# Attention and experts on one core: a unit's value products in two groups instead of three, a wider transposition of its maxima, and a new steady order

## The chip, the core and the metric

One Trainium2 chip, one of its cores. The time is device time of one execution in microseconds (us); lower is better. The kernel before took 1059.7 us (median of three runs, 1058.65 to 1059.89).

## What is computed

An attention layer whose output is the input of a mixture of eight experts, of which each token goes to one. Batch 8, 12 heads, 448 positions, head width 64; the experts have 768 inputs, 1024 hidden units and 768 outputs; 3584 tokens.

```
q_n, k_n = rmsnorm(q, g_q), rmsnorm(k, g_k)
scores = q_n @ k_n.T / sqrt(64);  scores -= scores.max(-1)
attn = exp(scores);  attn /= attn.sum(-1) + 1e-9
x = (attn @ v) with the heads side by side         # 3584 x 768
logits = x @ w_gate + modality_bias[modality_id]
e = argmax(logits);  g = softmax(logits)[e]
out[token] = g * (relu(x[token] @ w1[e]) @ w2[e])
```

## The kernel before, in words

**Units and slots.** The attention runs over 48 units; a unit is two heads of one batch. Both heads' 448 keys together are 896 rows, that is seven chunks of 128 (j = 0 to 6); chunk 3 holds the last 64 keys of the first head and the first 64 of the second. The main loop counts slots n = 7 u + j. In slot (u, j) the score products `st` of unit u for chunk j are issued (transposed: keys on partitions; two matmuls, four for chunk 3), and beside them work of other units: the products `sa` of unit u + 2, of which only the row maxima are wanted (queries on partitions, `PLAN['sa']` = 14 slots ahead); the turning `tr` of q and k of units three and four ahead; `mt`, which turns a unit's maxima; `av`, the products with the values of the unit before; `sums` and `gates`, which add the row sums of exp and the gate logits of four units in one PSUM tile `pm`; `sp` (in `recips`) and `xt`, which turn sums, logits and outputs back. `rt` are two small matmuls of the routing of a finished batch.

**What each engine has in a unit.** TensorE (PE): the above. ScalarE (ACT): exp of every `st`, the casts of turned q and k into their places, squares for the norms, copies of `av` and `pm`. VectorE (DVE): a maximum for every `sa` tile, the low halves of q and k (the products run in fp32r with a high and a low part), one product-add of the row sums, the scaling of `xt`, the routing. GpSimd (POOL): the rest of the row sums (`csum`), the two norms, and routing DMAs. SyncE issues loads and the moves of the halves.

**Value products.** For unit u, `av(u, c)` with c = 0, 1, 2 takes whole chunks: per head a 128 x 64 weight tile, head 0 writes output rows 0 to 63 and head 1 rows 64 to 127, so the array works as two halves of 64 columns. c = 3 takes the two halves of chunk 3, with 64 rows and 64 columns each. The numbers are fp32, so each of these matmuls shows as two in the trace: four `MATMUL` per c. `PLAN['av']` = (1, 1, 4, 6) says in which slot of the next unit each c is issued. One PSUM tile (`ps_o`, one buffer) takes them; `avcopy` on ACT empties it in the slot after c = 3.

**Maxima.** DVE writes the negated maxima of a unit into the seven columns of `mx`; `mt` (`PE.transpose(ps[0:NJ, :128], t["mx"], idn)`, L871) turns 128 x 7 into 7 x 128, ACT copies seven rows, a DMA moves them into the row of `ql` that subtracts them in the score products.

**Order.** Nothing is scheduled by a tool on these engines: `PLAN` says for every kind of work how many slots ahead of its unit it is issued (`tk`, `tq` turning; `nq`, `nk` norms; `sk`, `sq` squares; `rs` reciprocal roots; `ld` loads), `first` holds exceptions for the first units, `pdef` says in which of the next slots ACT's and DVE's parts of a `tr` come (even: at a slot's end, odd: at its start), `csd` and `cse` the same for the parts of `csum`, `pmp`/`pmpa` how many routing operations a slot takes, `sml` the slot of `sums` from unit 36 on, `xr`, `x0` and `w10` when tokens and weights of the first expert slot are fetched and turned. Each engine then does its instructions in that order, and semaphores make them wait for each other. PSUM has two buffers for `st`, two for `sa`, two that `tr`, `mt`, `xt`, `sp` and `rt` share.

**Experts.** Fourteen expert slots of 256 tokens follow: first products `ph` (144 matmuls of 256 columns), second products `py` (96 of 384), with steps 24 s + b; the table `MOE` says in which step which piece of the next slot's weights is fetched (`w1`, `w2`) or split into high and low part (`s1`, `s2`), and when its tokens are turned (`xtr`) and lists read (`get`, `fin`).

Of the kernel before, what the change touches and what calls it, by code (L numbers as in the profile page):

```python
# [13 lines left out]
ALU = mybir.AluOpType  # L14
# [7 lines left out]
NJ = 7  # L22
# [45 lines left out]
def kernel(  # L68
# [16 lines left out]
    PE, SY = nc.tensor, nc.sync  # L85
# [314 lines left out]
    def view(t, off, p, *dims):  # L400
        n = 1
        for d in dims:
            n *= d
        a = t[:p, off : off + n]
        if len(dims) > 1:
            ax = " ".join("abcd"[: len(dims)])
            a = a.rearrange(f"p ({ax}) -> p {ax}", **dict(zip("abcd"[1:], dims[1:])))
        return a
# [37 lines left out]
    sw, SS = at_g, W + LG  # L446
    ss_b, ry_b = ([view(sw, SS + 48 * (2 * o + i), CP, 2, 6 * NCH) for i in range(2)] for o in range(2))
    ra_b, rz_b = SS + 48 * 4, SS + 48 * 5
    mx_b = [view(sw, SS + 288 + 8 * i, 128, NJ) for i in range(2)]
    rs_b = [cp.tile([CP, NCH, 4, 2], F32, name=f"rs{i}") for i in range(2)]  # L450
    xt_0 = [view(r2w, o, 128, 2, TB) for o in (PW + VW + W, PW, PW + 512)]
    xg, xt_m = xrw[:, 0 : 2 * DM], view(xrw, 2 * DM, 128, 6, TB)
# [221 lines left out]

    if True:
        zt = view(yw, 0, 128, NE * NT * 2 // 128)
        for z in zeros + qm_b:
            V.memset(z.bitcast(F32), 0.0)
        HB = {}
# [188 lines left out]
        def mt(u):  # L868
            t = T[u]
            ps = ps_t.tile([128, 512], F32, tag="t", name=f"mt{u}")  # L870
            PE.transpose(ps[0:NJ, :128], t["mx"], idn)  # L871

            def act():
                ms = ms_b[u % 2]
                A.copy(ms, ps[0:NJ, :128])
                (A if u in PLAN["ma"] else SY).dma_start(t["ql"][64:65].rearrange("p h s -> p (h s)").bitcast(F32),
                            ms.bitcast(F32))

            return act
# [16 lines left out]
        def csum(u, h):  # L896
            t = T[u]
            if h == 0:
                t["cs"] = cs_b[u % 3]
            p = t["p"]  # L900
            c2 = c2_b[:, h]

            if h in CSV:
                V.scalar_tensor_tensor(out=c2, in0=p[:, 3], scalar=half[:, h : h + 1], in1=p[:, 4 * h],
                                       op0=ALU.mult, op1=ALU.add)
            else:
                G.tensor_tensor(out=c2, in0=p[:, 0], in1=p[:, 1], op=ALU.add)

            def more():
                if h in CSV:  # L910
                    G.tensor_tensor(out=c2, in0=c2, in1=p[:, 4 * h + 1], op=ALU.add)
                else:
                    G.tensor_tensor(out=c2[LO], in0=c2[LO], in1=p[LO, 3], op=ALU.add)

            def rest():
                G.tensor_tensor(out=t["cs"][:, h], in0=c2, in1=p[:, 4 * h + 2], op=ALU.add)

            return more, rest
# [610 lines left out]
```

## Time and profile before

| what | value |
|---|---|
| median of three runs | 1059.7 us |
| the profiled execution's own time | 1058.66 us |
| its span in the profile | 1056.9 us |
| TensorE busy | 1035.4 us, 98% |
| VectorE, ScalarE, GpSimd busy | 738.5, 698.5, 737.4 us |
| attention, first `st` to the first `ph` | 34.6 to 555.9 us |
| experts | 555.9 us to the end |

The profiled execution lies 1.0 us under the median, so a time that is reckoned from it stands 1 us lower than one reckoned from the median. A busy TensorE is one with a matmul somewhere in its pipeline; how fast it goes is read from the distance of one matmul's start to the next.

### The profile page before, as it was taken

How to read it: one execution, taken by the hardware profiler on the slowest of the kernel's cores; microseconds unless marked ns; L12 is line 12 of the kernel's file. 1: busy time of each engine (PE TensorE's matmuls, PEld its weight loads, DVE VectorE, ACT ScalarE, POOL GpSimd, SP SyncE). 2: the span in 40 equal slices, each digit the busy share in tenths (PEclk: the TensorE clock that was granted, in tenths of full speed). 3: DMA queues.
4: the chain of work that ended last, by engine and by line, in shares of the span. 5: the costliest groups of instructions: out<-in, count | busy, mean ns of one | idle time of the engine just before them, and what ended most of it. 6: DMA issues, size and time to landing. Idle time of an engine off the chain costs nothing.

```text
span 1056.9 us, 19700 instructions
## 1 busy us (share of the span) xinstructions
PE 1035.4 (98%) x6463; PEld 819.1 (78%) x6463; DVE 738.5 (70%) x1398; ACT 698.5 (66%) x1409; POOL 737.4 (70%) x743
## 2 busy tenths in 40 slices
PE   8899999999999999999999999999999999999996
PEld 7655566655666556665557999999999999999996
DVE  8787777877778777787687985756656665566640
ACT  6788888878888788887655554655555555555540
POOL 5897776787867878778876768665575556655531
PEclk8999999999999999999999999999999999999999
DMA  8766767787677877775735102111163111111170
GB/s 209 162 165 149 193 144 178 170 167 183 145 178 167 170 167 158 164 166 135 204 103 198 39 27 63 44 50 47 45 217 124 44 53 46 61 31 47 45 273 34
DMA packets 137156, 131.17 MB, mean 124 GB/s; under 512 B 75228, under 2 KB 130752, under 8 KB 135892
## 3 DMA queue, kind: packets, MB, share of 16 engines
q1 hardware_dynamic: 113188, 88.73, 36.1%
q0 software_dynamic: 23856, 41.08, 12.1%
q8 instruction: 53, 0.87, 0.4%
q14 instruction: 59, 0.48, 0.2%
HBM read 138.72 MB, written 22.38 MB: 152 GB/s over the span
## 4 chain that ended last, share of the span: by engine, by line
PE 86%; DVE 5%; DMA 2%; issue 2%; ACT 2%; POOL 1%; SPq 1%; POOLq 0%; ACTq 0%; DVEq 0%
PE ph L525 20%; PE py L556 19%; PE st L888 16%; PE av L927 15%; PE sa L860 5%; PE tr L773 3%; PE pm L942 2%; PE xt L984 2%; PE pm L949 1%; DMA l_d<-ltb,posi 1%; PE sa L851 1%; DVE w1w L53 1%; DVE at_hlw L53 1%; DVE w2lw L53 1%; DVE xw L53 1%
## 5 line engine op out<-in xcount | busy, mean ns | idle before, releaser
L53 DVE TENSOR_REDUCE at_hlw<-sa 128x1 f32<-128x448 f32 x336 | 203.2, 617 | 67.5 <-PE sa L860 64.6
L525 PEld LDWEIGHTS ph<-xw,w1w 128*128 128x128 f32 x2016 | 244.7, 192 | 4.1 <-issue 2.8
L525 PE MATMUL ph<-xw,w1w 128*128 128x256 f32 x2016 | 246.9, 284 | 0.6 <-DVE hlw L53 0.3
L888 PE MATMUL st<-w1w 128*128 128x448 f32 (+1 forms) x480 | 172.3, 408 | 2.3 <-ACT at_w2lw L53 2.0
L53 POOL DMA_INDIRECT xrw<-x_d,i x112 | 146.6, 1309 | 33.1 <-issue 31.7
L888 PEld LDWEIGHTS st<-w1w 128*128 128x128 f32 (+1 forms) x480 | 84.2, 189 | 102.6 <-ACT xw L53 38.1
L53 DVE TENSOR_TENSOR w1w<-r,w1w 128x512 fp32r<-128x512 f32 (+1 forms) x180 | 114.7, 678 | 15.7 <-ACT w1w L53 15.5
L53 ACT ACTIVATE r2w<-st 128x448 f32<-128x448 f32 x168 | 90.2, 539 | 52.6 <-PE st L888 46.6
L53 POOL TENSOR_TENSOR r2w<-r2w 128x448 f32<-128x448 f32 (+1 forms) x72 | 82.3, 1143 | 50.0 <-DVE r2w L53 21.5
L556 PE MATMUL py<-w2lw,hhw 128*128 128x384 f32 x448 | 115.0, 334 | 0.0
L53 ACT CAST w1w<-r 128x512 fp32r<-128x512 f32 (+1 forms) x180 | 103.1, 629 | 11.6 <-DMA r<-in_moe_w_dram,tb_w1i 8.5
L53 ACT ACTIVATE hhw<-ph 128x512 fp32r<-128x512 f32 x56 | 33.5, 598 | 114.6 <-PE ph L525 114.6
L53 ACT CAST w1w<-xw 64x448 fp32r<-64x448 f32 x188 | 105.7, 562 | 5.0 <-DVE xw L53 1.1
L860 PE MATMUL sa<-w1w 128*128 128x448 f32 x282 | 104.7, 373 | 3.4 <-DVE at_hlw L53 3.1
L53 ACT ACTIVATE at_w2lw<-st 128x448 f32<-128x448 f32 x168 | 90.3, 539 | 23.4 <-PE st L888 18.2
L888 PE MATMUL st<-w1w,w2ha 65*128 65x448 f32 x288 | 100.6, 370 | 0.0
L53 POOL DMA_INDIRECT out_dram<-yw,lb_oi x22 | 22.8, 1038 | 99.5 <-ACT yw L53 89.7
L53 POOL TENSOR_TENSOR xrw<-r,at_hlw 112x512 f32<-112x512 f32 x89 | 91.1, 1043 | 0.2
L556 PEld LDWEIGHTS py<-w2lw,hhw 128*128 128x128 f32 x448 | 81.0, 188 | 0.0
L53 POOL TENSOR_TENSOR r2w<-r2w,at_w2lw 64x448 f32<-64x448 f32 (+1 forms) x48 | 54.7, 1139 | 34.8 <-DVE rs L53 14.7
L53 DVE TENSOR_TENSOR w2lw<-r2w,w2ha 128x1536 fp32r<-128x1536 f32 x28 | 49.2, 1757 | 39.7 <-ACT w2ha L53 36.3
L53 DVE SCALAR_TENSOR_TENSOR hlw<-ph,hhw 128x512 fp32r<-128x512 f32 x56 | 38.6, 690 | 49.8 <-ACT hhw L53 47.0
(304 smaller groups left out, 2166.4 us busy)
## 6 DMA issues: line engine op xcount, KB each, us to landing
w1w<-xw SPq DMA_DIRECT2D x312, 112.0 KB
r<-in_q_dram SPq DMA_DIRECT2D x48, 224.0 KB
r<-in_k_dram SPq DMA_DIRECT2D x48, 224.0 KB
w2ha<-xw SPq DMA_DIRECT2D x72, 112.0 KB
r2w<-in_v_dram SPq DMA_DIRECT2D x24, 224.0 KB
at_w2lw<-in_v_dram SPq DMA_DIRECT2D x24, 224.0 KB
x_d<-at_w2hb SPq DMA_DIRECT2D x8, 672.0 KB
x_d<-yw SPq DMA_DIRECT2D x8, 672.0 KB
```

The source lines that it names most:

```text
L53: return fn(*a, **kw)
L525: PE.matmul(ps[:, i], lhsT=lt_, rhs=rt_[:, c], start=n == 0, stop=n == 17)
L556: PE.matmul(ps[n][:, :384], lhsT=lt_[:, j, 128 * t : 128 * t + 128], rhs=rt_[:, 384 * n : 384 * n + 384], start=j == 0 and m == 0, stop=j ...
L773: PE.transpose(sp[:, c], src[:, c], idn[:CP, :CP])
L851: PE.matmul(ps[:, :S], lhsT=qm_b[u % 2], rhs=hi_b[u % 2][1], start=True, stop=True)
L860: PE.matmul(ps[:, :S], lhsT=t["qq"][:, h, a : a + 128], rhs=t["kk"][h], start=True, stop=True)
L888: PE.matmul(ps[:, :S], lhsT=l, rhs=t["qq"][:, h] if first else t["ql"][:, h], start=first and (j != 3 or h == 0), stop=not first and (j != ...
L927: PE.matmul(t["av"][64 * h : 64 * h + 64, :S], lhsT=vv[r, u % 3, j], rhs=t["p"][r, j], start=c == 0, stop=c == 3)
L942: PE.matmul(R[g][32 * i : 32 * i + 32, :S], lhsT=sel[:, m], rhs=T[u + i // 2]["cs"][:, i % 2], start=m == 0, stop=False, tile_position=(0, ...
L949: PE.matmul(sm[32 * i : 32 * i + 32, :S], lhsT=wg[:, (4 * g + i) % NP], rhs=T[4 * g + i]["xt"], start=False, stop=True, tile_position=(0, ...
L984: PE.transpose(ps[:CP, 128 * c : 128 * c + 128], T[u]["xt"][:, c * CP : (c + 1) * CP], idn)
```

## The change

The table `PLAN` moves c = 3 of the value products from slot 6 to slot 4, where c = 2 already is; with it a good many other entries move by a slot or more. `mx` becomes 72 columns wide (columns 7 to 71 are set to zero once by GpSimd), and `mt` turns all 72. The two edits in `csum` change nothing at these settings (`csv` stays (1,)), and `xq` is read nowhere. In `MOE` some forty pieces of the expert slots 0 to 5 are issued at other steps, most of them one to six later.

```
-'av': (1, 1, 4, 6), 'cse': (2, 1), 'rc': 6, 'sml': 4, 'rtj': 6, 'xr': (0, 3, 5), 'w10': (40, 24, 18), 'x0': 31,
+'av': (1, 1, 4, 4), 'cse': (4, 2), 'rc': 9, 'sml': 2, 'rtj': 2, 'xr': (0, 4, 5), 'w10': (28, 24, 18), 'x0': 28,
-'nq': 28, 'nk': 28, 'sk': 49, 'rs': 48, 'ld': 58, 'pdef': ((0, 1, 2, 0), (0, 1, 2, 0)),
+'nq': 29, 'nk': 31, 'sk': 48, 'rs': 47, 'ld': 59, 'pdef': ((0, 0, 3, 0), (1, 2, 2, 1)),
-'pmp': (0, 0, 1, 1, 1, 0, 1), 'pmpa': (1, 0, 1, 0, 1, 1, 1),
+'pmp': (0, 0, 2, 1, 2, 0, 1), 'pmpa': (0, 0, 1, 0, 0, 1, 2),
...
-('s1', 4, 1): 73, ('s1', 4, 3): 70, ('s1', 4, 5): 91, ('s1', 2, 6): 42, ('s1', 2, 10): 37, ('xtr', 3, 0): 59, 'fin0': 6,
+('s1', 4, 1): 79, ('s1', 4, 3): 76, ('s1', 4, 5): 97, ('s1', 2, 6): 45, ('s1', 2, 10): 45, ('xtr', 3, 0): 62, 'fin0': 2,
...
-    mx_b = [view(sw, SS + 288 + 8 * i, 128, NJ) for i in range(2)]
+    mx_b = [view(sw, SS + 288 + 72 * i, 128, 72) for i in range(2)]
...
+        G.memset(sw[:, SS + 288 : SS + 432], 0.0)
...
-            PE.transpose(ps[0:NJ, :128], t["mx"], idn)
+            PE.transpose(ps[0:72, :128], t["mx"], idn)
...
-                G.tensor_tensor(out=c2, in0=p[:, 0], in1=p[:, 1], op=ALU.add)
+                G.tensor_tensor(out=c2, in0=p[:, 4 * h], in1=p[:, 4 * h + 1], op=ALU.add)
...
-                    G.tensor_tensor(out=c2[LO], in0=c2[LO], in1=p[LO, 3], op=ALU.add)
+                    r = (LO, HI)[h]
+                    G.tensor_tensor(out=c2[r], in0=c2[r], in1=p[r, 3], op=ALU.add)
```

**Place 1: TensorE, slots 4 to 6 of unit 24** (names carry the unit; `av23` are the value products of unit 23). Before:

```order
L984 MATMUL xt18_3568<-idn_65,at_w2lw_163 112x128 x4
L927 MATMUL av23_3520<-at_w2lw_163 64x448 x2
L942 MATMUL pm_151<-at_w2lw_163,sel_75 32x448 x2
L942 MATMUL pm_151<-at_w2hb_162,sel_75 32x448 x2
...
L773 MATMUL tr28_1_3598<-idn_65,xrw_156 128x112 x4
L927 MATMUL av23_3520<-at_w2lw_163 64x448 x2
L1037 MATMUL rt2_3605<-oh2_3363,ones_70 128x32
L1038 MATMUL rt2_3605<-oh2_3363,tri_72 112x32
L888 MATMUL st25_0_3621<-w1w_157 128x448
```

The same place now:

```order
L986 MATMUL xt18_3574<-idn_65,at_w2lw_163 112x128 x4
L929 MATMUL av23_3520<-at_w2lw_163 64x448 x4
L944 MATMUL pm_151<-at_w2lw_163,sel_75 32x448 x2
L944 MATMUL pm_151<-at_w2hb_162,sel_75 32x448 x2
...
L774 MATMUL tr28_1_3612<-idn_65,xrw_156 128x112 x4
L889 MATMUL st25_0_3626<-w1w_157 128x448
```

The last pair of value products stands behind the third; `tr` and the next unit's first `st` follow each other; the routing's `rt` is now in slot 2. The order holds 47 such pairs (units 0 to 46) before and none now; unit 47's eight stand in one row in both.

**Place 2: GpSimd, unit 26 to 27** (`r2w` and `at_w2lw` hold exp, written `r2w` the running sum, `at_w2hb`/`at_hhw` a unit's finished sums of one head, `xrw` the norms of q and k). Before:

```order
L53 TENSOR_TENSOR r2w_159<-r2w_159 128x448
L53 TENSOR_TENSOR r2w_159<-r2w_159 64x448
L53 TENSOR_TENSOR at_hhw_164<-r2w_159 128x448
L53 TENSOR_TENSOR r2w_159<-r2w_159 128x448
L53 TENSOR_TENSOR at_hhw_164<-r2w_159 128x448
L53 TENSOR_TENSOR xrw_156<-r1_2_155,at_hlw_165 112x2x4x64 x2
```

And now:

```order
L53 TENSOR_TENSOR r2w_159<-r2w_159 128x448
L53 TENSOR_TENSOR r2w_159<-r2w_159 64x448
L53 TENSOR_TENSOR xrw_156<-r1_2_155,at_hlw_165 112x2x4x64
L54 DMA l_d_64<-ltb_119,posi3_4067 28672x2
L53 TENSOR_TENSOR xrw_156<-r1_2_155,at_hlw_165 112x2x4x64
L53 TENSOR_TENSOR at_hhw_164<-r2w_159 128x448
L53 TENSOR_TENSOR r2w_159<-r2w_159 128x448
L53 TENSOR_TENSOR at_hhw_164<-r2w_159 128x448
```

The two norms stand ahead of the last three parts of the row sums instead of behind them.

**Place 3: ScalarE, the last unit** (`xw<-r2w` is the cast of a third of the first expert slot's tokens, which waits for DVE's transposition; `st47` are exps, `av46` the copy of the value products). Before:

```order
L53 ACTIVATE at_w2lw_163<-st47_3_6448 128x448
L53 CAST w1w_157<-r1_1_154 128x256
L53 CAST xw_158<-r2w_159 128x512
L53 ACTIVATE at_w2lw_163<-st47_4_6463 128x448
L53 CAST w1w_157<-r1_2_155 128x256
L53 ACTIVATE at_w2lw_163<-st47_5_6477 128x448
```

And now:

```order
L53 ACTIVATE at_w2lw_163<-st47_3_6454 128x448
L53 CAST w1w_157<-r1_1_154 128x256
L53 ACTIVATE at_w2lw_163<-st47_4_6466 128x448
L53 CAST w1w_157<-r1_2_155 128x256
L53 COPY xrw_156<-av46_6426 128x448
L53 CAST xw_158<-r2w_159 128x512
L53 ACTIVATE at_w2lw_163<-st47_5_6480 128x448
```

The exp of chunk 4 no longer stands behind the second of these casts; the exp of chunk 5 does.

## Rows read from the trace of the kernel before

**Rows 1.** Stretches: length, busy us (instructions) of PE, PEld, DVE, ACT, POOL; clock, DMA, GB/s.
```profile
100.00:500.00 400.00, 399.33 (x2173) 242.63 (x2176) 310.42 (x675) 329.44 (x730) 315.60 (x338) 1.00 0.72 165
554.40:557.80 3.40, 3.40 (x12) 2.00 (x13) 2.61 (x10) 2.06 (x6) 0.00 (x0) 0.50 0.03 1
660.00:1020.00 360.00, 360.00 (x2554) 360.00 (x2553) 226.76 (x301) 197.54 (x290) 219.51 (x181) 1.00 0.24 76
```

**Rows 2.** Timeline of PE within a unit: start, us, what it did (x matmuls).
```profile
305.20 0.37 PE L860 MATMUL sa<-w1w 128*128 128x448 f32 x1
305.41 0.27 PE L871 MATMUL mt<-idn,at_hlw 128*7 128x128 f32 x1
305.61 1.72 PE L927 MATMUL av<-r2w 128*64 128x448 f32 x8
307.27 0.47 PE L888 MATMUL st<-w1w 128*128 128x448 f32 x1
307.58 0.37 PE L888 MATMUL st<-w1w,w2ha 65*128 65x448 f32 x1
307.79 0.37 PE L860 MATMUL sa<-w1w 128*128 128x448 f32 x1
308.00 0.55 PE L773 MATMUL tr<-idn,xrw 112*128 112x112 f32 x4
308.31 0.65 PE L888 MATMUL st<-w1w 128*128 128x448 f32 x2
...
310.03 0.60 PE L984 MATMUL xt<-idn,at_w2hb 128*112 128x128 f32 x4
310.56 0.97 PE L927 MATMUL av<-r2w 128*64 128x448 f32 x4
311.47 0.57 PE L949 MATMUL pm<-at_hhw,wg 128*32 128x448 f32 x2
```

**Rows 3.** Timeline of PE, the unit before that: the last pair, in slot 6.
```profile
302.26 0.55 PE L773 MATMUL tr<-idn,xrw 112*128 112x112 f32 x4
302.74 0.97 PE L927 MATMUL av<-at_w2lw 64*64 64x448 f32 x4
303.64 0.41 PE L1037 MATMUL rt<-oh,ones 112*128 112x32 f32 x2
```

**Rows 4.** Timeline of PE: the last unit's value products, all c in one go.
```profile
559.11 3.38 PE L927 MATMUL av<-at_w2lw 128*64 128x448 f32 x16
562.42 0.86 PE L525 MATMUL ph<-xw,w1w 128*128 128x256 f32 x5
```

**Rows 5.** Operations of DVE and POOL, 100 to 500 us: count, busy, mean ns, idle before.
```profile
L53 DVE TENSOR_REDUCE at_hlw<-sa 128x1 f32<-128x448 f32 x255 | 154.0, 617 | 41.9 <-PE sa L860 41.7
L53 POOL TENSOR_TENSOR xrw<-r,at_hlw 112x512 f32<-112x512 f32 x73 | 74.7, 1043 | 0.0
```

**Rows 6.** Timeline of DVE at a change of unit.
```profile
325.37 0.61 DVE L53 TENSOR_REDUCE at_hlw<-sa 128x1 f32<-128x448 f32 x1
325.90 0.17 DVE L54 RECIPROCAL ltb<-pm 112x4 f32<-112x4 f32 x1
...
327.32 0.67 DVE L53 SCALAR_TENSOR_TENSOR xw<-tr,gs,xw 128x448 fp32r<-128x448 f32 x1
327.91 0.67 DVE L53 SCALAR_TENSOR_TENSOR r2w<-r2w,half 128x448 f32<-128x448 f32 x1
328.51 0.67 DVE L53 TENSOR_REDUCE at_hlw<-xrw 112x8 f32<-112x512 f32 x1
```

**Rows 7.** Timeline of POOL there; in brackets the wait and its cause.
```profile
328.73 1.13 POOL L53 TENSOR_TENSOR r2w<-r2w 128x448 f32<-128x448 f32 x1 [4.44 <-DVE r2w L53]
```

**Rows 8.** Timelines of ACT and PE in the last unit.
```profile
552.15 0.62 ACT L53 CAST xw<-r2w 128x512 fp32r<-128x512 f32 x1 [1.90 <-DVE r2w L53]
553.27 0.67 PE L888 MATMUL st<-w1w 128*128 128x448 f32 x2 [1.63 <-ACT at_w2lw L53]
```

**Rows 9.** Waits of PE's weight loads, 560 to 700 us: us, times, longest.
```profile
PEld ph L525 <- DVE w1w L53: 0.7, 2, 0.5
```

More of the change, by code (lines that the diff above doesn't have):

```diff
@@ new lines @@
+PLAN = {'rtj': 2, 'rushat': 36, 'av': (1, 1, 4, 4), 'xt': 4, 'xte': (2, 6), 'sm': 4, 'la': 4, 'rc': 9, 'csv': (1,), 'csj': (3, 6), 'csd': (1, 1), 'cse': (4, 2), 'sa': 14, 'mt': 6, 'tk': 22, 'tq': 19, 'nq': 29, 'nk': 31, 'sk': 48, 'sq': 50, 'rs': 47, 'ld': 59, 'first': {('sq', 0): -22, ('sk', 0): -22, ('nk', 0): -20, ('nq', 0): -19, ('sq', 1): -21, ('sk', 1): -20, ('sq', 2): -20, ('sk', 2): -18, ('nk', 1): -16, ('nq', 1): -14, ('tk', 0): -18, ('tq', 0): -18, ('sa', 0): -15, ('tk', 1): -15, ('tq', 1): -13, ('sa', 1): -3, ('mt', 0): -5, ('tk', 2): -7, ('tq', 2): -7, ('nq', 2): -11, ('nk', 2): -13, ('nq', 3): -6, ('nk', 3): -5, ('sq', 3): -11, ('sk', 3): -8, ('sq', 4): -7, ('sk', 4): -10, ('sq', 6): -5, ('sk', 6): -2, ('sk', 7): -6, ('sq', 8): 6, ('sk', 8): 5, ('nk', 7): 22, ('tq', 3): 0, ('mt', 1): 1, ('nq', 5): 12, ('mt', 8): 50, ('rs', 0): -21, ('rs', 2): -17, ('nq', 8): 35, ('rs', 5): -6, ('mt', 2): 8, ('nq', 7): 19, ('mt', 5): 29, ('mt', 6): 36, ('nq', 6): 14, ('sa', 5): 20, ('rs', 8): 10, ('mt', 4): 22, ('nk', 4): 2, ('tk', 5): 13, ('tk', 3): -1, ('tk', 4): 6, ('tq', 4): 11, ('ld', 1): -22, ('ld', 2): -21, ('ld', 3): -17, ('ld', 4): -19, ('ld', 5): -21, ('tk', 8): 35, ('sa', 3): 7, ('mt', 3): 18, ('tq', 8): 38, ('nk', 9): 38, ('ld', 6): -18, ('nk', 5): 3, ('sa', 2): 0, ('sq', 5): -15, ('tk', 7): 30, ('tq', 7): 31, ('nq', 4): -3, ('sa', 7): 35, ('tk', 6): 20, ('sq', 9): 19, ('nk', 6): 17, ('sa', 6): 28, ('tq', 9): 45, ('nk', 8): 28, ('sk', 5): -12, ('tq', 5): 15, ('ld', 8): -4, ('sq', 7): -2, ('rs', 1): -19, ('ld', 7): -11, ('tq', 6): 23}, 'rs0': {0: 0, 1: 1, 2: 2, 5: 0, 8: 0}, 'sastep': {3: 1, 4: 1, 1: 0.5, 2: 1, 0: 1}, 'start': -22, 'warm': {5: 4, -6: 14, -18: 1, -17: 4, -19: 1, 4: 1, 3: 1, -5: 1, -22: 7, -11: 6}, 'warmn': 1, 'early': 1, 'late0': 1, 'pmp0': 2, 'ramp': 10, 'pmp': (0, 0, 2, 1, 2, 0, 1), 'nv': [(5, 0), (8, 0), (8, 1), (1, 1), (6, 1), (2, 1), (0, 0)], 'pmpa': (0, 0, 1, 0, 0, 1, 2), 'rush': (1, 1, 1), 'ps': [(3, 0), (8, 1), (9, 1), (6, 1)], 'pa': [(5, 1), (5, 0), (9, 0), (7, 0)], 'rtr': 3, 'sml': 2, 'vs': [(7, 1), (1, 0), (0, 1)], 'vr': [(0, 8)], 'va': [(1, 0), (1, 1), (6, 1), (3, 1), (4, 1), (4, 0), (0, 1), (2, 0)], 'ma': [], 'gain': -21, 'lv0': 3, 'lv1': -9, 'lg': -2, 'parts': {(0, 1): (1, 5, 8, 2), (0, 0): (1, 2, 5, 4), (1, 1): (0, 3, 11, 5), (2, 1): (0, 2, 5, 0), (3, 0): (1, 4, 2, 5), (1, 0): (0, 9, 5, 5), (5, 0): (1, 7, 2, 9), (4, 1): (0, 4, 5, 6), (8, 1): (1, 1, 3, 3), (7, 0): (1, 2, 3, 1), (5, 1): (0, 7, 2, 1), (6, 1): (0, 2, 4, 1), (7, 1): (0, 1, 2, 0), (3, 1): (0, 4, 2, 1), (8, 0): (0, 1, 3, 2), (2, 0): (0, 2, 2, 2), (4, 0): (0, 1, 0, 0), (6, 0): (0, 0, 2, 2)}, 'w10': (28, 24, 18), 'x0': 28, 'xr': (0, 4, 5), 'pdef': ((0, 0, 3, 0), (1, 2, 2, 1)), 'nvd': (), 'gc': -12, 'kh': (-16, -7, -7, 3), 'zt': -7, 'pg': (6, 3), 'xq': 1}
```

3 lines of the change are left out of this document (1 added, 2 removed).

## The prediction

> **What bounds the kernel now.** I read the stretches first [rows 1]. From 100 to 500 us TensorE has a matmul in its pipeline for 399.33 of 400 us, while DVE, ACT and POOL work 310, 329 and 316 us; from 660 to 1020 us it is busy all the time at the full clock, and the others are at 55 to 63%. So the question in both halves is how closely TensorE's matmuls follow each other. How long a unit takes comes from the count of maxima, seven a unit [rows 5]: 255 / 7 = 36.4 units in 400 us, 10.98 us each. In one of them DVE works 8.52, ACT 9.04 and POOL 8.66 us, each the busy time of rows 1 over 36.4. That is the cover that other work has: about 2 us a unit, less on ACT.
>
> Then the timeline of TensorE [rows 2, 3]. The starts are to be read, not the durations: within a run of full-width matmuls a 448-column product starts every 0.21 us (307.58 to 307.79 to 308.00). Around the value products the distances are larger. Four turnings `tr` and then `st`: 0.31 us from the first `tr` to the `st` (308.00 to 308.31). The same four and then value products: 0.48 (302.26 to 302.74). So entering costs 0.17. Leaving: the second matmul of the first `st` comes 0.31 us after the first instead of 0.21 (307.27 to 307.58), 0.10 more. Third, a group has a price of its own: eight matmuls take 1.66 us (305.61 to 307.27), four take 0.91 (310.56 to 311.47), so four more cost 0.75 and a group has 0.16 besides. Once the first units are through, TensorE stops for others in few places; the longest stop is in the last unit [rows 8].
>
> **The merge.** The last pair c = 3 moves from slot 6 behind c = 2 in slot 4. No matmul is saved. What goes is one entry and one exit, 0.17 + 0.10 = 0.27 us. Does the group's own 0.16 go as well? The last unit has all four c in one go [rows 4]: sixteen matmuls in 3.31 us (559.11 to 562.42). Eight steps of two at 0.375 are 3.00; the rest, 0.31, is twice 0.16 although it is one group. The place where the form changes from 128*64 to 64*64 costs as much as a group's end, and c = 3 alone takes 0.90 [rows 3], like c = 2 alone. So the 0.16 stays.
>
> The Trainium skill has a rule for this (TensorEngine Tiling (Array Packing), Key Properties): changing the tiling mode, "not just tile", drains the engine. It speaks against the change, since c = 2 and c = 3 are two modes and the drain between them stays. The trace agrees, with the 0.31 that is left over; without the rule one would reckon 0.43 a unit.
>
> The order has 47 such pairs. 47 x 0.27 = 12.7 us. Five of them are followed by the routing's small matmuls instead of an `st`, where I count no exit: 12.2. Bounds: the entry alone, 47 x 0.17 = 8.0; with the group's price, 47 x 0.43 = 20.2.
>
> **Sums in slot 2.** From unit 36 on, `sums` (five pairs of units, 37 to 45) leave the group in slot 4 and stand alone in slot 2. There they enter and leave anew: 5 x 0.27 = 1.4 us back, at most 5 x 0.43 = 2.2. They need the row sums of the unit before, whose last part POOL now issues a slot later; if it comes late TensorE waits up to one POOL operation, 1.13 us [rows 7], five times: 5.7 at the worst, which I leave to the rivals.
>
> **The wider transposition.** `mt` streams the same 128 columns. A seven-column `mt` begins 0.21 us after its `sa` (305.20 to 305.41) and the value products 0.20 after it; a 112-row `tr` begins 0.21 after its `sa` too. There is nothing to gain in 48 of them and nothing to lose: 0, with 47 x 0.17 = 8 on the gaining side as the bound if they did hide an entry. The set-to-zero is one POOL operation before the loop, beside the first loads: 0, at most the 1.04 us of a norm, the nearest row [rows 5].
>
> **The steady order.** Slots 5, 6, 0 and 1 now follow each other without value products between them, and this is where the others can come late. TensorE goes from the end of the group to the `sa` of slot 1 in 0.72 + 0.93 + 0.62 + 0.41 = 2.7 us (three products of 0.21 a slot, 0.10 for the exit, 0.31 for a `tr`). That `sa` needs the buffer whose maximum is the second of the stretch. A maximum takes 0.53 us in a queue, the two product-adds 0.60 each and the squares' sum 0.67 [rows 6]. The second maximum is done some 1.6 us after the group's end, 0.5 for the first product to come out included. The next limit is the `sa` of slot 2: its buffer needs the third maximum, behind both product-adds and the squares: 0.5 + 3 x 0.53 + 1.2 + 0.67 = 4.0, against 2.7 + 0.21 + 0.20 + 1.66 + 0.41 = 5.2. Both have about 1.1 us left. Routing operations, 0.17 us and more apiece, eat that in a unit or two of each batch. On ACT, `avcopy` leaves the stretch between chunk 6 and chunk 1, which is shortened by 1.17, and 0.53 goes with it. On POOL the norms, 2 x 1.04, move into the wait of 4.44 us that POOL has now for DVE [rows 7]. Nothing takes an engine over its 10.7 us a unit. I set 1.5 us in all for new waits; bounds -1 (the short ones of now gone) and 8 (0.4 in every second unit).
>
> **The end of the attention.** In the last unit ACT's cast of the tokens waits 1.90 us for DVE, the exp of chunk 4 is queued behind it, and TensorE waits 1.63 [rows 8]. Behind that stop the granted clock is 0.50 from 554.4 to 557.8, the 1.2 GHz level, and full again after [rows 1]; work of 3.4 us that would take 1.7. Now the cast stands behind that exp and before the next one. DVE has as much to do as before, so the wait may only move to the first expert product. I take half of 1.63 + 1.7: -1.7; between -3.3 and +2 (another such stop).
>
> **The experts.** After 660 us TensorE never stops [rows 1]: the moves can only lose there. Before it, it waits 0.7 us for splits [rows 9]. Pieces of slot 4 come six steps later, a step of second products being six matmuls, and stand next to the turning of its tokens. I take -0.3; between -0.7 and +3.
>
> **Sum**, against the profiled execution's 1058.66: -12.2 + 1.4 + 1.5 - 1.7 - 0.3 = -11.3, 1047.4. The median lies 1.0 above that execution; I put half of it on: **1048.0**.
>
> **Rivals.**
> 1. *DVE or ACT becomes late in the short stretch in every unit.* For: the stretch loses 1.17 us, and ACT has 9.04 of 10.7 us to do. Against: 1.1 us of margin reckoned above. It decides when more than 1.1 us of other work stands in DVE's part of it. Price 0.4 in about half of the 39 steady units, 8 us instead of 1.5: 1054.5.
> 2. *POOL becomes the bound; slower.* Norms now stand ahead of the parts of the row sums and need reciprocal roots that are issued one slot later, in every third unit, while the norms come three slots earlier. POOL does everything in order; if it waits there for ACT's roots as long as it now waits for DVE, 4.44 us [rows 7], it has 8.66 + 4.44 = 13.1 us of a unit of 10.7, and the exp buffers, which wait for its sums, pass 2.4 on. From 2.0 us of wait on it decides. In 13 units 31 us: 1048 + 31 = 1079. Against: the roots' inputs are there a slot earlier and a wait of 2 us leaves no mark.
> 3. *The wider `mt` saves an entry.* If seven columns put the array into a mode of its own and 72 do not, 47 x 0.17 = 8.0: 1040. Against: the 0.21 and 0.20 above, which are those of a 112-wide turning. The Trainium skill lists modes by width, down to 32 columns, and says that column tiling excludes the transpose mode for fp32 (same page, Available Configurations and Restrictions); the second agrees with the row, which shows no drain.
> 4. *The late pieces stop TensorE at expert slots 1 to 4 or a second time at the end of the attention.* +2 and +3 instead of -1.7 and -0.3: 1055. For: DVE's queue there is full; against: three quarters of the experts run without a wait.
>
> **Chances.** Forecast 0.65 (own range 1043 to 1052), rival 1 0.15, rival 2 0.05, rival 3 0.05, rival 4 0.10. The range 1042 to 1056 holds the forecast, rivals 1 and 4, and leaves out 2, 3 and the outer parts of the first. About 0.2% (2 us) is what a measurement of this kernel can tell from no change. Faster: all but rival 2 and the far ends of 1 and 4, 0.90; within 0.2%: 0.05; slower: 0.05.
>
> **What would show it.** Right: a unit without `sums` takes TensorE 0.27 us less from one chunk-0 `st` to the next; no entry in slot 6; `av` sixteen or eight matmuls with the 0.16 between the forms still there. The attention ends some 11 us earlier and the experts take as long. Wrong: waits of TensorE on DVE's maxima or ACT's exps in slots 0 to 2 of most units (rival 1), on `pm` or exps behind POOL (rival 2), `mt` followed by value products in under 0.20 us (rival 3), or a stretch at half clock where none was (rival 4).

## The result: 1.4% slower, and the profile after

The changed kernel takes 1076.2 us (median of four runs, 1073.1 to 1076.84) against 1059.8 for the kernel before beside it: ratio 1.0142, 95% interval [1.012, 1.0164]. The prediction was 1048.0, range 1042 to 1056. The profiled execution took 1076.78 us, its span is 1075.0.

Where the time went, from the first `st` of units 0, 9, 36 and 47, and to the end, in the two traces (us):

| stretch | before | after |
|---|---|---|
| units 0 to 8 | 93.5 | 95.5 |
| units 9 to 35 | 297.0 | 299.1 |
| units 36 to 46 | 118.9 | 125.8 |
| unit 47 and the experts | 512.8 | 519.5 |

The stretches of [rows 1], columns as there; the second is the one of half clock, which is no longer at the end of the attention:

```profile
100.00:500.00 400.00, 393.58 (x2149) 239.14 (x2145) 316.29 (x652) 328.71 (x722) 312.73 (x335) 1.00 0.69 162
653.00:656.60 3.60, 3.60 (x18) 3.60 (x19) 2.23 (x2) 1.97 (x3) 2.99 (x3) 0.53 0.08 3
660.00:1020.00 360.00, 360.00 (x2550) 360.00 (x2549) 226.68 (x300) 195.56 (x285) 227.22 (x184) 1.00 0.22 66
```

TensorE had a matmul for 399.33 of these 400 us before and has one for 393.58 now, while DVE works 6 us more. From 660 to 1020 us TensorE is busy all the time in both.

Four rows of the view of TensorE's waits in the whole changed kernel (us, times, longest), and the row of the kernel before that answers to the first:

```profile
PE sa L861 <- DVE at_hlw L53: 9.3, 13, 3.2
PE ph L525 <- ACT at_w2lw L53: 1.6, 1, 1.6
PE ph L525 <- ACT w1w L53: 1.3, 1, 1.3
PE pm L944 <- DVE rmx L54: 0.9, 1, 0.9
```

```profile
PE sa L860 <- DVE at_hlw L53: 3.1, 2, 2.9
```

`sa` waits until DVE has taken the maximum of the tile that holds its buffer. The rows that answer to [rows 2, 3], TensorE's timeline of the changed kernel, at the start of unit 21 and later in it, where nothing waits:

```profile
262.56 0.55 PE L774 MATMUL tr<-idn,xrw 112*128 112x112 f32 x4
262.88 0.45 PE L889 MATMUL st<-w1w 128*128 128x448 f32 x1
263.16 0.37 PE L889 MATMUL st<-w1w,w2ha 65*128 65x448 f32 x1
263.37 0.37 PE L861 MATMUL sa<-w1w 128*128 128x448 f32 x1
...
269.78 0.60 PE L986 MATMUL xt<-idn,at_hhw 128*112 128x128 f32 x4
270.31 1.87 PE L929 MATMUL av<-r2w 128*64 128x448 f32 x8
272.12 0.56 PE L951 MATMUL pm<-at_hhw,wg 128*32 128x448 f32 x1
```

The merged group takes 1.81 us (270.31 to 272.12), twice the 0.90 of a single one: the 0.16 between the two forms stayed, as forecast. `tr` is followed by `st` after 0.32 instead of by value products after 0.48. But the second matmul of that `st` still comes 0.28 behind the first (262.88 to 263.16), where a running product comes after 0.21.

Then a place where TensorE waits 1.1 us: DVE, GpSimd (POOL) and TensorE of the changed kernel, unit 17:

```profile
218.60 0.61 DVE L53 TENSOR_REDUCE at_hlw<-sa 128x1 f32<-128x448 f32 x1
219.19 1.06 POOL L53 TENSOR_TENSOR xrw<-r,at_hlw 112x512 f32<-112x512 f32 x1
219.22 2.60 DVE L53 SCALAR_TENSOR_TENSOR r2w<-r2w,half 128x448 f32<-128x448 f32 x1
220.19 1.14 POOL L53 TENSOR_TENSOR at_w2lw<-r2w 128x448 f32<-128x448 f32 x1
221.75 0.67 DVE L53 SCALAR_TENSOR_TENSOR xw<-tr,gs,xw 128x448 fp32r<-128x448 f32 x1
222.34 0.67 DVE L53 TENSOR_REDUCE at_hlw<-xrw 112x8 f32<-112x512 f32 x1
222.94 1.14 DVE L53 TENSOR_REDUCE at_hlw<-sa 128x1 f32<-128x448 f32 x2
223.60 0.47 PE L861 MATMUL sa<-w1w 128*128 128x448 f32 x1 [1.14 <-DVE at_hlw L53]
```

The product-add of head 1's row sum took 0.67 us in [rows 6]. Here it takes 2.60: as long as GpSimd works through a norm and the last part of head 0's sum (to 221.33), plus 0.49. Of the product-adds between 100 and 540 us 8 of 40 took over 0.71 us in the kernel before, up to 2.27, and 20 of 39 do now: the durations of this one form, which the prediction did not look at, showed the stretching already. The next maximum, which stands behind it, starts 4.3 us after the last one, and TensorE's `sa` waits 1.14 for it. In [rows 7] GpSimd stands idle there, waiting for this very product-add: the 4.44 us into which the prediction moved the norms at no cost.

### The profile page after: what moved, and what is told of

Read it like the earlier page. It is cut to its first block, busy times and chain, and to the rows that moved or that the text cites. A ratio compares the mean times of both kernels' runs of the same rounds, so it can differ in the third digit from the quotient of the medians.

```text
span 1075.0 us, 19707 instructions
## 1 busy us (share of the span) xinstructions
PE 1037.9 (97%) x6463; PEld 819.3 (76%) x6463; DVE 753.8 (70%) x1398; ACT 702.2 (65%) x1409; POOL 740.3 (69%) x744
## 4 chain that ended last, share of the span: by engine, by line
PE 73%; DVE 12%; DMA 5%; ACT 4%; issue 2%; POOL 2%; SPq 1%; POOLq 0%; DVEq 0%; ACTq 0%
PE ph L525 20%; PE py L556 19%; PE av L929 11%; PE st L889 11%; PE sa L861 4%; DVE at_hlw L53 3%; PE tr L774 2%; DVE r2w L53 2%; PE pm L944 2%; DVE xw L53 1%; DMA w1w<-xw 1%; PE xt L986 1%; ACT w1w L53 1%; DVE w1w L53 1%; DMA r<-in_k_dram 1%
## 5 line engine op out<-in xcount | busy, mean ns | idle before, releaser
L525 PE MATMUL ph<-xw,w1w 128*128 128x256 f32 x2016 | 249.5, 285 | 5.4 <-ACT at_w2lw L53 1.6
```

Source lines behind the costliest of these rows:

```text
L525: PE.matmul(ps[:, i], lhsT=lt_, rhs=rt_[:, c], start=n == 0, stop=n == 17)
```

## The experiments

Each kernel ran beside the kernel before. Units 9 to 35 and the product-adds' sum are from the profiled run, the product-adds of 100 to 540 us (39 or 40 of them). "Steady waits" are TensorE's waits of more than 0.15 us from 128 to 410 us. Seven more kernels (e9 to e12, e14 to e16) are not in the table: while they ran, the kernel before beside them took 1076 to 1117 us, and theirs took 1102 to 1115 in the median, with 544 to 560 us from unit 47 on, so of them the attention alone is used.

| kernel | median | ratio, 95% | units 9-35 | 36-46 | product-adds |
|---|---|---|---|---|---|
| before | 1060 | 1 | 297.0 | 118.9 | 31.1 |
| changed | 1076.2 | 1.0142 [1.012, 1.0164] | 299.1 | 125.8 | 44.8 |
| e1 merge alone | 1072.5 | 1.0107 [1.0078, 1.0136] | 303.8 | 120.8 | 29.6 |
| e2 changed, GpSimd back | 1071.6 | 1.0102 [1.0064, 1.014] | 295.1 | 124.4 | 29.2 |
| e3 GpSimd moved alone | 1072.9 | 1.0125 [1.0101, 1.0149] | 299.5 | 122.3 | 39.4 |
| e8 norms moved alone | 1062.9 | 1.0029 [1.0008, 1.005] | 296.7 | 119.4 | 35.6 |
| e5 changed, one input | 1066.5 | 1.0052 [1.0033, 1.0071] | 292.9 | 124.6 | 24.3 |
| e6 merge, squares moved | 1073.4 | 1.0112 [1.0079, 1.0146] | 303.0 | 119.4 | 32.3 |
| e4 changed, experts back | 1075.1 | 1.0126 [1.0092, 1.0161] | 299.2 | 128.2 | 44.4 |
| e18 changed, sums back | 1071.8 | 1.0117 [1.009, 1.0144] | 299.2 | 124.3 | 41.9 |
| e19 GpSimd and sums back | 1065.7 | 1.0053 [1.0034, 1.0073] | 294.0 | 122.0 | 31.3 |
| e7 those and experts back | 1067.3 | 1.0061 [1.0037, 1.0085] | 294.1 | 121.4 | 29.7 |
| e17 merge to unit 34 only | 1061.8 | 1.0014 [0.9998, 1.003] | 295.9 | 119.3 | 31.9 |

**The merge alone (e1).**

```
before: -'av': (1, 1, 4, 6)   +'av': (1, 1, 4, 4)
```

> The kernel before with one entry changed: the last pair of value products in slot 4 ('av' (1, 1, 4, 4)); nothing else moves. Theory P (a shared way into SBUF: DVE's product-add of the row sums, which reads two operands from SBUF, stands still while GpSimd's additions run, and the new order puts GpSimd's norms and the last part of head 0's row sum beside it): the merge itself is sound, so -12 us less a little for new waits: 1048 to 1050, and the 39 product-adds between 100 and 540 us still take some 31 us. Theory D (the short stretch of slots 5 to 1 leaves DVE and ACT too little time, whatever GpSimd does): TensorE waits for maxima as in the changed kernel, and the gain is eaten: 1058 or more.

12 us slower: theory P, with which I started, is not the whole cause. Some 4 of them stand in unit 47 and the experts (516.8 against 512.8). Units without a wait are 0.19 us shorter (11.00 to 10.81, 10.10 to 9.91). But there are waits where the kernel before has none, here the steady ones of e1:

```profile
PE sa L860 <- DVE at_hlw L53: 3.6, 7, 1.0
PE rt L1037 <- DVE xw L53: 2.1, 2, 1.0
PE st L888 <- DMA w1w<-xw: 1.9, 1, 1.9
```

The same view of the kernel before has no row at all. DVE's timeline in e1, and the `sa` that waits:

```profile
196.81 0.59 DVE L53 TENSOR_REDUCE at_hlw<-sa 128x1 f32<-128x448 f32 x1
197.32 0.88 DVE L54 TENSOR_REDUCE pm<-lg 112x32 f32<-112x384 f32 x1
198.11 0.67 DVE L53 SCALAR_TENSOR_TENSOR xw<-tr,gs,xw 128x448 fp32r<-128x448 f32 x1
198.70 0.67 DVE L53 SCALAR_TENSOR_TENSOR r2w<-r2w,half 128x448 f32<-128x448 f32 x1
199.30 0.68 DVE L53 TENSOR_REDUCE at_hlw<-xrw 112x8 f32<-112x512 f32 x1
199.89 0.18 DVE L54 TENSOR_TENSOR pm<-pm,ball 112x32 f32<-112x32 f32 x1
199.99 0.61 DVE L53 TENSOR_REDUCE at_hlw<-sa 128x1 f32<-128x448 f32 x1
200.66 0.48 PE L860 MATMUL sa<-w1w 128*128 128x448 f32 x1 [0.35 <-DVE at_hlw L53]
```

No product-add is stretched here. Between two maxima lie a routing operation of 0.88, two product-adds, a sum of squares and another routing operation: 3.18 us from start to start, more than the shortened stretch covers. That is rival 1 of the prediction. But the two longest waits for maxima in e1, 0.88 and 0.98 of the 3.6, do stand behind a stretched product-add (1.96 us at 219.38, 2.07 at 355.05): with GpSimd's order as before, the shorter units alone put these two beside a GpSimd addition. And 1.9 of the 7.6 is one wait for a DMA.

**GpSimd's order back (e2) and moved alone (e3, e8).**

```
e2, changed: -'nq': 29, 'nk': 31, 'cse': (4, 2)   +'nq': 28, 'nk': 28, 'cse': (2, 1)
e3, before:  -'nq': 28, 'nk': 28, 'cse': (2, 1)   +'nq': 29, 'nk': 31, 'cse': (4, 2)
e8, before:  -'nq': 28, 'nk': 28                  +'nq': 29, 'nk': 31
```

> The changed kernel with the norms and the last part of head 0's row sum at their slots of before ('nq' 28, 'nk' 28, 'cse' (2, 1), and the exception for unit 9). Theory P: the product-adds take 31 us between 100 and 540 us instead of 44.8, most waits of TensorE for maxima in units 9 to 45 go, and of the 20.7 us of new waits in the attention 12 to 16 come back: 1060 to 1064; what is left is the experts' +7 and some waits on the sums. Theory D, and theory Q (the changed slots of DVE's parts of the turnings and of the routing, 'pdef' and 'pmp', put other work ahead of the maxima): within 3 us of 1076.

> The kernel before with only those three entries changed to the new ones ('nq' 29, 'nk' 31, 'cse' (4, 2)); the value products stay in three groups. Theory P: the product-adds stretch as in the changed kernel (some 45 us instead of 31 between 100 and 540 us); the stretch of slots 5 to 1 is 1.17 us longer than in the changed kernel, so fewer of them reach TensorE: slower by 3 to 8 us, 1063 to 1068. Theory D: 1060 within 2 us. Theory Q: the same, 1060.

> The kernel before with the norms alone moved ('nq' 29, 'nk' 31), head 0's last part left where it was. Theory P (DVE's product-add stands still beside GpSimd's additions): the norms are half of the work that now lies beside it: product-adds between 100 and 540 us take 33 to 37 us in all (31 before, 39.4 with both moved), and the time is between 1060 and 1066. If the norms in their new slots wait for the reciprocal roots instead, GpSimd shows waits for ACT of 2 us and more in every third unit and the time is above 1070.

e2: the product-adds are back at 29.2 us and the steady waits for maxima fall from 5.0 us to 1.0. The span to unit 47 is 7.3 us shorter, but unit 47 and the experts take 2.1 longer, and the median is only 4.6 lower (its runs scatter from 1067.7 to 1075.9): less than the 12 expected. e3 and e8: about half of the stretching comes with the norms, as expected (35.6, then 39.4, from 31.1). In time e8 is 0.3% slower, as expected, and e3 1.2%, more than expected (1072.9 against 1063 to 1068). But in e3's profiled run, its fastest (1065.6), the steady waits for maxima are 0.4 us. So the stretched product-adds hardly reach TensorE's maxima with three groups; what made e3's other runs 1072 to 1076 isn't shown, and GpSimd's move may cost by another way too.

**One input instead of two (e5).**

```
-V.scalar_tensor_tensor(out=c2, in0=p[:, 3], scalar=half[:, h : h + 1], in1=p[:, 4 * h], op0=ALU.mult, op1=ALU.add)
+V.tensor_reduce(out=c2, in_=p[:, 4 * h].unsqueeze(2), op=ALU.add, axis=AX.X)
```

> The changed kernel, its order untouched, but the product-add on DVE reads one operand from SBUF instead of two: a reduction over an axis of length one, 448 elements in and out; it leaves out the addition of chunk 3, so the row sums of head 1 are short. Theory P: no such instruction is stretched (each about 0.62 to 0.68 us) although GpSimd runs the same additions beside it, and 12 to 16 us come back: 1060 to 1064. A narrower form of it, that GpSimd's queue order delays something else (exp buffers, norms), and theories D and Q: within 3 us of 1076.

The order of all engines is the changed kernel's; the second operand from SBUF is gone, and with it the addition of chunk 3 and the kind of operation. By operation, 100 to 540 us (count | busy, mean ns): the kernel before, the changed kernel, then e5:

```profile
L53 DVE SCALAR_TENSOR_TENSOR r2w<-r2w,half 128x448 f32<-128x448 f32 x20 | 15.3, 766 | 0.0
L53 DVE SCALAR_TENSOR_TENSOR r2w<-at_w2lw,half 128x448 f32<-128x448 f32 x20 | 15.8, 788 | 0.0
```

```profile
L53 DVE SCALAR_TENSOR_TENSOR r2w<-r2w,half 128x448 f32<-128x448 f32 x20 | 26.3, 1313 | 0.0
L53 DVE SCALAR_TENSOR_TENSOR r2w<-at_w2lw,half 128x448 f32<-128x448 f32 x19 | 18.5, 976 | 0.0
L53 DVE SCALAR_TENSOR_TENSOR xw<-tr,gs,xw 128x448 fp32r<-128x448 f32 x38 | 25.8, 678 | 4.0 <-ACT xw L53 3.8
```

```profile
L53 DVE TENSOR_REDUCE r2w<-r2w 128x448 f32<-128x448 f32 x20 | 12.2, 609 | 0.0
L53 DVE TENSOR_REDUCE r2w<-at_w2lw 128x448 f32<-128x448 f32 x20 | 12.2, 608 | 0.0
```

None is stretched, though GpSimd runs the same additions beside them, and 9.7 us come back (12 to 16 were expected). Steady waits for maxima: 0.7 us. That it is not the kind of operation shows in the last row of the changed kernel: the same operation with its first operand from PSUM (`tr`) and one from SBUF takes 678 ns, and 12 of these 38 began while a GpSimd addition ran, none over 0.69 us. So it is the second operand from SBUF, not GpSimd's order as such. The Trainium skill says so (SBUF — State Buffer, Who interferes with whom): a DVE instruction with two SBUF inputs contends with a GpSimd instruction that reads SBUF, and such contention is an exclusive lock. The traces agree: 2.60 us beside two GpSimd additions, 0.61 with one input; and DVE's reductions of scores, which read PSUM, stay at 617 ns in both kernels.

Units 9 to 35 of e5 take 4.1 us less than before, near the 5.1 that the merge gives in 27 units; what e5 still loses stands behind them, 5.7 us in units 36 to 46 and 6.1 from unit 47 on.

**Three groups in the changed order (e11, e16).**

```
changed: -'av': (1, 1, 4, 4)   +'av': (1, 1, 4, 6)
```

> The changed kernel with the last pair of value products back in slot 6 ('av' (1, 1, 4, 6)), everything else new. By the merge's own price it would be 8.9 us slower than the changed kernel, 1085. If its waits come mostly from the short stretch (theory D), they go with it and cancel this: 1070 to 1077, product-adds between 100 and 540 us still stretched to some 40 us. If the stretched product-adds (theory P) reach TensorE whatever the length of the stretch: 1080 or more.

> The changed kernel with the last pair of value products back in slot 6 ('av' (1, 1, 4, 6)), everything else new; the earlier run of it was disturbed, and in its attention units 9 to 35 took 298.75 us and TensorE's waits there 5.4 us instead of 13.1. If both mechanisms are needed for the loss (stretched product-adds reach TensorE only in the short stretch), the merge's 8.9 us come back as cost and some 8 to 12 us of waits go: 1072 to 1078, the same as the changed kernel. If the stretched product-adds alone make it, 1080 or more.

Both runs are of the same kernel, and their times say nothing (above). The product-adds are stretched to 50 us in sum (49 in e16), and yet, steady waits of e11:

```profile
PE sa L861 <- DVE at_hlw L53: 0.9, 2, 0.5
PE st L889 <- DMA w1w<-xw: 0.6, 1, 0.6
PE sa L861 <- DMA w1w<-xw: 0.3, 1, 0.3
```

So in the changed order the steady waits for maxima are 0.9 with GpSimd moved alone (e11, and e16 too), 1.0 with the merge alone (e2) and 5.0 with both. Either alone is nearly covered; together they aren't. The fourth corner, three groups and GpSimd as before in the changed order, was not run; the kernel before, which has none of these waits, has the old order. Units 9 to 35 of e11 take 298.8, so with GpSimd moved the merge's 27 x 0.19 = 5.1 us came to nothing (299.1). In e16 they take 303.5; the 4.7 more stand in unit 28 alone, where `sa` waits 2.3 for a DMA.

**Which order would feed the merge (e6, e12, e9, e10, e15).**

```
e6, before:  +'av': (1, 1, 4, 4), 'ld': 62, 'sq': 55, 'sk': 52
e12, before: +'av': (1, 1, 4, 4), 'pdef': ((0, 0, 3, 0), (1, 2, 2, 1))
e9, before:  as e12, and 'pmp', 'pmpa', 'rtj', 'rc', 'w10', 'x0' of the changed kernel; e10 has e6's entries too
e15, before: 'av' c = 3 in slot 4 in units 9, 12, 13, 16, 18, 20, 21, 24, 25, 28, 30, 32, 33 only
```

> The kernel before with the merge alone, as in the run before, and besides the squares of q and k taken out of the short stretch: 'sq' 55, 'sk' 52, 'ld' 62, so that DVE's two sums of squares (0.67 us each) stand in slots 2 and 5 behind the value products, when DVE has no scores to take maxima of, not in slots 0 and 1. Theory D (the merge alone lost because DVE's queue in slots 5 to 1 holds more than the shortened stretch): TensorE's waits for maxima in units 9 to 45 fall from 8.9 us to 3 or less, and the merge's own 10 us show: 1050 to 1055, faster than before. If the loss has another source (ACT's exps, the moves of the halves by DMA, GpSimd), it stays near that run: 1068 to 1073.

> The kernel before with the merge and only 'pdef' of the changed kernel (DVE's product-add ahead of its part of the turned k, the rest of k's and q's parts a slot earlier or later). If DVE's order is what the merge alone lacked, units 9 to 35 take 294 to 297 us (303.8 with the merge alone) and the time is 1056 to 1062. If it is the amount of work in the short stretch, whatever its order: 300 us and more there, 1066 to 1073.

> The kernel before with the merge and the changed kernel's places for DVE's and ACT's parts of the turnings and for the routing ('pdef', 'pmp', 'pmpa', 'rtj', 'rc', and 'w10' and 'x0', which the lists' time asks for); GpSimd's order, the sums, the roots, loads, squares and the experts are those of before. The merge by itself takes 0.19 us from a unit without waits (11.00 to 10.81 and 10.10 to 9.91 in both the changed kernel and the merge alone), 8.9 in all. If DVE's places are what the merge alone lacked: units 9 to 35 take some 294 us (297.0 before, 303.8 with the merge alone), the experts as long as before, and the time is 1053 to 1057. If the merge can't be fed by any of these orders: 1062 and more, with TensorE waiting for maxima or for exps in units 9 to 35.

> The same with the squares of q and k out of the short stretch as well ('sq' 55, 'sk' 52, 'ld' 62). If DVE's sums of squares still stood ahead of late maxima, units 9 to 35 take some 292 us and the time is 1 to 3 us below the run without this, 1051 to 1055. In the run with the merge and the squares alone there were new waits, for the moves of halves (DMA) and of ACT's exps for GpSimd's roots (units 17 and 22); if these come from the earlier loads and squares, it is slower than the run without this by 3 us and more.

> The kernel before with the merge in only 13 of the units 9 to 33: those whose maxima had no wait in the run with the merge alone, that is those in which DVE has no routing in slots 5 to 1. Theory D: each of them is 0.19 us shorter and nothing waits anew: units 9 to 35 take 294.5 us instead of 297.0, 1057 to 1058, faster than before by 0.2%. If any shortened stretch costs, wherever it is: 1060 or more.

e6 was a miss, 1073.4: maxima wait less than in e1 (2.2 us steady against 3.6), moves by DMA more (2.8 against 1.9), the routing as long (2.0 against 2.1). e12's units 9 to 35 take 301.6: the order of DVE's parts alone is not it. e9 (300.4, of which 4.0 stands in unit 28 alone) and e10 (296.0) come nearer to the 294 and 292 expected, but miss them, and their units 36 to 46 take 128 us; the outputs of both are not the layer's, and why isn't shown. e15 is a miss that teaches: its units 9 to 35 take 300.2 instead of 294.5. The merged units are mostly 0.15 to 0.20 shorter, and an unmerged one behind them 0.54 to 0.61 longer (units 10, 14, 22, 26: 11.5 to 11.6 instead of 10.99), with `sa` late in its slot 2.

**Sums and experts (e4, e18, e19, e7).**

```
e4, changed:  'MOE' and 'xr' of before
e18, changed: -'sml': 2   +'sml': 4
e19, changed: 'nq', 'nk', 'cse', 'sml' of before;   e7: as e19, and 'MOE' and 'xr'
```

> The changed kernel with the table of the expert slots and the slots of the first tokens' turning of before ('MOE' and 'xr'); the attention is that of the changed kernel. If the moved pieces themselves cost the experts' 6.7 us, the stops of TensorE before ph and py (at some 565 to 617 and at 650 us in the changed kernel) go and it is 5 to 7 us faster than the changed kernel: 1069 to 1071. If the experts only inherit a late DVE and GpSimd from the end of the attention, it stays within 2 us of 1076.

> The changed kernel with the sums of units 37 to 45 back in slot 4 ('sml' 4). By the prediction's term 1.4 us come back, 1074 to 1075. By the three-group runs in the changed order (units 36 to 46: 4.9 us over before, nearly all in even units) it is 4 to 5 us: 1070 to 1073, and the waits of TensorE before pm in units 38 and 46 are gone.

> The changed kernel with GpSimd's order and the sums as before, and the experts' table and token turning ('MOE', 'xr') new. The run that had these back too took 1067.3, and from the last unit's first scores to the end 516.5 us (512.9 before, 519.5 in the changed kernel). If the table costs what the experts lost, 3 to 6 us more than that run: 1070 to 1073, with TensorE's stops before ph at some 605 and 640 us; if the experts only inherited the late attention, 1066 to 1069.

> The changed kernel with three things as before: GpSimd's order (norms and head 0's last part, 'nq', 'nk', 'cse'), the experts ('MOE', 'xr') and the sums in slot 4 ('sml' 4). What stays new: the merge, the wider transposition, DVE's and ACT's parts of the turnings, the routing's pace, roots, squares and loads by one slot. If the parts are about additive, 7 us (GpSimd, by the first start of the last unit's scores in the run that had it alone), 6 us (experts) and 2 us (sums) come off: 1060 to 1063, no faster than before. If DVE's new places are what the merge needs and the losses lay in these three alone: 1050 to 1055.

The experts' table is innocent: with that of before 1075.1 against 1076.2, and 1067.3 (e7) against 1065.7 (e19) with the new one. e7 missed both of its expected ranges, 1060 to 1063 and 1050 to 1055. The sums in slot 2 cost 4.4 us (e18) and 5.9 (e19 against e2) by the medians, but in both pairs the intervals overlap; by the traces it is 1.5 and 2.4 us in units 36 to 46, where they stand. e18's profiled run was its slowest; its other four are 1071.2 to 1073.6.

**The merge where it can be fed (e14, e17).** e14 is e7 with three groups and `pdef` of before from unit 35 on; e17 is the kernel before with the merge, `pdef` and `rc` of the changed kernel up to about unit 34, and its `pmp`, `pmpa`, `rtj` and slots of `rs`, `sk`, `ld` throughout.

> The run with three parts as before (GpSimd's order, experts, sums; 1067.3), and besides from unit 35 on three groups and 'pdef' of before. Units 9 to 34 keep the merge and DVE's new places: some 294 us there. Units 36 to 46 took 121.4 us in that run and 118.9 before: without the merge there the waits go, 119 to 120, and the last unit's wait with them: 1058 to 1063. If the last twelve units lose by the routing's later rush and the earlier tokens ('rushat' 36, 'x0' 28), 1065 to 1068.

> The kernel before with the merge and the changed kernel's places for DVE, routing, roots, squares and loads up to unit 34 only; from there on three groups and everything as before, GpSimd's order and the experts as before throughout. Units 9 to 35 took 294.1 and 295.0 us in the two runs with this steady order, 297.0 before. If the last twelve units and the experts are those of before again: 1056 to 1059, faster than both. If the change from one order to the other costs what it gains: 1060 to 1064.

e14, one of the seven: units 9 to 35 in 295.0, 36 to 46 in 121.4, as long as in e7. So three groups there bring nothing back; e17, which has the routing's rush and the first tokens as before, takes 119.3. e17: 1061.8 us, ratio 1.0014 [0.9998, 1.003], no gain: 1.2 us less in units 9 to 35, 3.0 more in units 0 to 8 and 2.0 from unit 47 on. No version here beats the kernel before.

## Why the prediction was wrong

- *The merge, -12.2.* The mechanism was there, the size was not: 0.19 us a unit, 47 x 0.19 = 8.9. The entry, 0.16, went. The exit, 0.10, didn't: the first `st` behind a `tr` pays 0.08 of it as well (262.88 to 263.16), which [rows 2] show in slot 2: the two matmuls of the `st` behind a `tr`, at 308.31, span 0.65 where one takes 0.37. The 0.16 between the forms stayed, as forecast.
- *The steady order, +1.5.* This step failed, twice. "Both have about 1.1 us left" counted DVE's fixed work and set the routing aside as "0.17 us and more apiece" in "a unit or two of each batch"; e1 has one routing operation of 0.88 in the stretch, waits of more than 0.15 us in 9 of the units 9 to 35, in 8 of them for DVE, and is 12 us slower with the merge alone. And "on POOL the norms ... move into the wait of 4.44 us" took idle time of GpSimd for free: the instruction it waited for runs on DVE, and beside GpSimd's additions it takes up to 2.60 us instead of 0.67 (giving this back is worth 9.7 us in e5; in e2 4.6 in the median, 7.3 in the trace to unit 47). Rival 1 (0.15) named the place and the engine, but not this cause, and its 8 us came on top of a gain that was too large.
- *Rival 2 (POOL late for the roots)* did not happen: the 74 norms between 100 and 540 us have 1.0 us of idle time before them in all. That its time, 1079, lies near the measured one is luck.
- *Sums in slot 2, +1.4.* Measured 1.5 and 2.4 us by the traces, 4.4 and 5.9 by the medians (e18, e19), which do not settle it. The wait that was left to the rivals ("up to one POOL operation") is part of it: in unit 46 `pm` waits 0.92 for DVE, and in e2 1.03 for GpSimd.
- *The wider transposition, 0*: right; `mt` to `av` is 0.20 in both.
- *End of the attention, -1.7*: the stretch of half clock left 554 us and came back at 653, behind stops of 1.32 and 0.27 before `ph`. Nothing was gained.
- *The experts, -0.3*: they took 6.7 us longer, but not by their table (e4, e7 against e19). The stops stand before `ph` at 565 to 570 us, before `py` at 599 to 601, and before `ph` at 614 to 617 and 651 to 653. Kernels of the table with the merge in the last units have this stretch at 516 to 522 us, those with three groups there at 512 to 515 (before, e3, e8, e17), and e1, the merge alone, at 516.8. Which wait hands it on is open.

So against the sum of -11.3 the traces show: 3.3 less from the merge; some 6 us in units 9 to 35 from the stretched product-adds that the short stretch does not cover (299.1 against 292.9 in e5); in units 36 to 46, 6.9 us longer than before, 1.5 to 2.4 from the sums' place, 1.2 to 1.4 from GpSimd's order (e5, e2) and the rest open; 6.7 in unit 47 and the experts, of which 4.0 come with the merge alone (e1); and 2.0 in units 0 to 8, open as well. With GpSimd's order and the sums as before (e19) units 9 to 35 are 3.0 us shorter than in the kernel before, and the loss that is left, 1065.7, stands in units 0 to 8, 36 to 46 and from 47 on. The parts overlap, and the medians scatter by 2 to 4 us; a finer split is not shown.

## What to carry to other kernels

Before an operation is moved into another engine's idle time, ask what that engine waits for: if it waits for an instruction that reads two operands from SBUF on DVE, an addition on GpSimd put beside it takes its time from that instruction. Look for it in the durations of that one instruction: it counts as busy time there, not as a wait. A merge that shortens a stretch of TensorE has to be reckoned at the engine that must keep up in that stretch, with its rare work (here the routing) put in unit by unit, and the exit of a group read from what stands there afterwards, not from what stood there before.

## What was not expected of the hardware

- A 128x448 product-add with both operands in SBUF took 0.67 us alone and up to 2.60 in the changed kernel beside GpSimd's `TENSOR_TENSOR`s, ending some 0.5 us after the last of them; GpSimd's own took their usual 1.06 and 1.14. In all traces but e5's, 234 of the 751 product-adds between 100 and 540 us took over 0.71 us (up to 3.18), and every one of them ended 0.48 to 0.50 us after a `TENSOR_TENSOR` of GpSimd. The 410 beside which GpSimd did nothing took 0.65 to 0.71, and so did the 52 beside nothing but its DMA issues.
- The second matmul of the first full product follows the first after 0.28 us behind a transposition and after 0.31 behind value products; in a running row it follows after 0.21.
